# Layer 0 of a two-layer attention and MLP kernel: which tiles are transposed where, and when weight pieces are loaded

## The chip, the cores and the metric

The kernel runs on one core of a Trainium2 chip. The core has five engines that run side by side, each through its own list of instructions in order: TensorE (PE; its weight loads are shown as a separate row, PEld), VectorE (DVE), ScalarE (ACT), GpSimd (POOL) and SyncE (SP), which here only issues DMAs. They are held together by semaphores. The metric is the device time of one execution in microseconds (us), lower is better: 882.56 us, the median of three runs (882.15 to 882.82).

## The reference

`x` is 2048 rows of 448 numbers. Two layers with the same weights follow one another; in each

```
y   = layernorm(x);  q, k, v = split(y @ wqkv)            # 16 heads of 28
pq  = phi(q); pk = phi(k)                                  # phi(t) = (t+1 if t>0 else exp(t)) + 1e-6
kv  = sum over rows of pk^T v;  z = sum over rows of pk    # per head
x   = x + ((pq @ kv) / (pq . z + 1e-6)) @ wo
x   = x + gelu(layernorm(x) @ w1 + b1) @ w2 + b2           # w1: 448 x 1792, w2: 1792 x 448
```

The attention is linear: nothing of it is 2048 x 2048, but `kv` and `z` need all rows before the first output row can be made.

## The kernel before, in words

**Tiles and phases.** The rows are cut into 16 tiles of 128. A layer has three phases. Phase 1 takes the tiles one by one: normalise, project to k and q, and add k^T times the normalised rows into four accumulators (`G`; v itself is never formed). Phase 2 (`ORDER`, L494) makes from them the small matrices for the output and does the first block of four tiles. Phase 3 is the MLP of each block of four tiles, with the attention output of the next block woven in.

**Two pieces per number.** All large products are made from fp32 split in a rounded high piece and the remainder, each product being three matmuls (hi*hi, hi*lo, lo*hi). The split of a tile or a weight is a copy on ACT and a subtraction on DVE or POOL. A group `K`, `Q` or `G` of one tile is 11 matmuls of 448 columns.

**How a tile gets transposed.** The projections need the tile with its columns on the partitions. There are two ways. With `t < TURNED[l]` (L374), TensorE does it: `stage_b` (token `T`) issues four 128x128 transposes into a PSUM bank with tag `h`, which the q projection also uses, and `stage_x` (token `X`) splits it, ACT `XH` (L251) and DVE `XL` (L252). ACT first has to make a copy of the last 64 columns, twice (`tail`, L387). With `t >= TURNED[l]` the tile is "turned": DVE transposes blocks of 32x32 into a `sq` tile shared by two rows' tiles (`turn`, L277 and L278; tokens `tu`, or `v7` for tile 7), SP stores that to DRAM (`store_sq`, L283), and after the store has landed SP reads it back in four permuted DMAs (`spread`, L289, token `sp`); `stage_x` then splits the result, ACT `XH` (L295) and DVE `XL` (L296). Before, tiles 0 to 5 of layer 0 go through TensorE and 6 to 15 are turned. Layer 1 turns all of its tiles.

**The order is written by hand.** Phase 1 is a list of steps, one per tile; `STEPS` (L502) gives the tokens of a step, `STEP` (L501) the default. A token's instructions go to their engines' queues in that order. In step t: `K` and `Q` project tile t, `T` and `X` transpose and split tile t+1, `G` accumulates tile t-1, `qp` finishes q of tile t-1 and stores it, `kp`, `kh`, `kl` finish k, `s` splits the normalised tile for `G`. `a`, `n` are the statistics (with a power on POOL, L203) and the normalisation, for the tiles that `NORM[0][t]` lists, or for the tile in the token (`a5`). `ld` loads x up to the last tile of `NORM[0][t+2]`. Steps 9 to 15 have no `Q`: those q projections fill phase 2.

**Weights in the background.** In layer 0, w1 and w2 arrive in 32 pieces, 20 of them in phase 1. Token `bg` calls `background(n, m)` (L359): it first splits up to m pieces that are waiting (ACT copy L341, L344 or L352, then POOL subtraction L342, L345 or L353), then has SP issue n more loads. A piece lands in one of two buffers (`stg`), so a load waits in SP's queue until the POOL subtraction of the piece two before it is done. All DMAs of the kernel are in SP's one queue, in the order of the tokens: behind such a load wait the x loads, the spreads, the stores of q, and at the end of phase 1 the loads of `pq` that phase 2 starts with. `BG` (L523) is n for each step.

**Phase 2 begins** with `Q ld1 z ld0 ld2 qz0 qz1 G gt qs1 Q Qp kv qs0 tq1 ...`, ahead of which `background(0)` splits what is still waiting. `z` is a matmul and an ACT operation (`zb`, L622); `gt` four ACT copies of the accumulators (L632); `qz` a product of `pq` and `zb` on POOL (L693); `qs` a DVE chain (L699 to L704); `kv` 32 matmuls (L640); `tq1` the first transposes of `pq` (L711).

Of the kernel before, what the change touches and what calls it, by code (L numbers as in the profile page):

```python
# [9 lines left out]
F32 = mybir.dt.float32  # L10
# [12 lines left out]
def linear_attn_mlp_kernel(  # L23
# [12 lines left out]
    pe, act, dve, pool, sp = nc.tensor, nc.scalar, nc.vector, nc.gpsimd, nc.sync  # L36
# [8 lines left out]
    G = 112  # L45
# [6 lines left out]
    work = ctx.enter_context(tc.tile_pool(name="work", bufs=2))  # L52
# [136 lines left out]


    def ln_bn(xs):
        st = work.tile([128, 6], F32, name="bst", tag="bst", bufs=2)
        dve.bn_stats(st, xs)
        return st

    def ln_stats(xs, st=None):
        st = ln_bn(xs) if st is None else st
        mv = work.tile([128, 2], F32, name="bmv", tag="bmv", bufs=2)
        dve.bn_aggr(mv, st)
        ve = work.tile([128, 1], F32, name="bve", tag="bve", bufs=2)  # L200
        dve.tensor_scalar(ve, mv[:, 1:2], 1e-5, None, op0=OP.add)  # L201
        rs = work.tile([128, 1], F32, name="brs", tag="brs", bufs=2)
        pool.tensor_tensor(rs, ve, mhalf, op=OP.pow)  # L203
        return xs, mv, rs

# [28 lines left out]
    def block(key):  # L234
        if key not in blocks:
            blocks[key] = Block()
        return blocks[key]
# [10 lines left out]
    def split_x(key, j):  # L248
        tp = tps.pop((key, j))
        hi, lo = blocks[key].pieces(j)  # L250
        act.copy(hi, tp)  # L251
        dve.tensor_sub(lo, tp, f(hi))  # L252
# [19 lines left out]
    def turn(x, key, t):  # L272
        x = x[:, :D]
        if (key, t // 2) not in squares:
            squares[key, t // 2] = half("sq")
        sq = squares[key, t // 2].rearrange("p (m c u n) -> p c m u n", m=4, c=4, n=32)[:, :, :, t % 2]
        dve.transpose(sq[:, :3], x[:, :TL].rearrange("p (c m n) -> p c m n", c=3, n=32))  # L277
        dve.transpose(sq[:, 3].rearrange("p (u m) n -> p u m n", u=2),  # L278
                      x[:, TL:].rearrange("p (m n) -> p m n", n=32)[:, None].to_broadcast([128, 2, 2, 32]))
# [44 lines left out]
    def bg_pieces():  # L324
        n = 0

        def stage():
            nonlocal n
            n += 1
            if n <= LATE:  # L330
                return t512("xn", 2, "stg")[:, :D]
            return t448(f"W{5 + n % 2}", 1, "stg")

        for fc in range(4):
            sl = slice(fc * D, (fc + 1) * D)
            for c in range(4):
                s = stage_piece(w1[:, sl], c, sp, stage())

                def go(c=c, s=s, sl=sl):
                    if c < 3:  # L340
                        act.copy(w1h[:, c, sl], s)  # L341
                        pool.tensor_tensor(w1l[:, c, sl], s, f(w1h[:, c, sl]), op=OP.subtract)  # L342
                    else:
                        act.copy(w1x[:, sl], s)  # L344
                        pool.tensor_tensor(w1x[64:128, sl], s[64:128], f(w1x[64:128, sl]), op=OP.subtract)  # L345
                yield go
        for i in range(NF):
            s = stage()
            sp.dma_start(s, w2[i * 128:(i + 1) * 128, :])

            def go(i=i, s=s):
                act.copy(w2h[:, i], s)  # L352
                pool.tensor_tensor(w2l[:, i], s, f(w2h[:, i]), op=OP.subtract)  # L353
            yield go

    bg = bg_pieces()
    bg_wait = []

    def background(n, m=NF):  # L359

        for g in bg_wait[:m]:
            bg_wait.pop(0)()
        for _ in range(n):
            g = next(bg, None)
            if g is not None:
                bg_wait.append(g)
# [4 lines left out]
    sts = {}  # L371


    TURNED = (6, 0)  # L374
    tails = {}

    def stage_a(l, t):
        sts[l, t] = ln_stats(xt.pop((l, t)))

    def stage_n(l, t):  # L380
# [3 lines left out]
        xns[l, t] = xs  # L384
        if t < TURNED[l]:
            d = tails[l, t] = work.tile([128, 128], F32, name="tail", tag="tail", bufs=2)
            act.copy(d.rearrange("p (u n) -> p u n", u=2), xs[:, None, TL:].to_broadcast([128, 2, 64]))  # L387

    def stage_t(l, t):
        if t >= TURNED[l]:  # L390
            turn(xns[l, t], ("a", l, t // 4), t % 4)
            if t % 2:
                store_sq(("a", l, t // 4), t % 4 // 2)

    def stage_sp(l, t):
        if t >= TURNED[l]:
            block(("a", l, t // 4))
            spread(("a", l, t // 4), t % 4 // 2)

    def stage_b(l, t, tag="h"):  # L400
        if t < TURNED[l]:
            transpose_x(xns[l, t], tails.pop((l, t)), ("a", l, t // 4), t % 4, tag)

    def stage_x(l, t):
        key = ("a", l, t // 4)
        if t < TURNED[l]:
            split_x(key, t % 4)
# [67 lines left out]
    def stage_g(l, t, acc):  # L475
# [26 lines left out]
    STEPS = {  # L502
# [8 lines left out]
    }  # L511
    NORM = (
        ((2,), (3,), (5, 6), (7,), (8, 9), (10,), (11,), (12,), (13,), (14,), (15,)),
        ((5,), (6,), (7,), (8,), (9,), (10,), (11,), (12, 13), (14,), (15,)),
    )

# [3 lines left out]
        "qa1 qb1 qa2 qb2 Q00 Q10 Q01 Q11 Q02 Q12 s0 a2 kp0 qa3 qb3 kh0 n2 kl0 kp1 Q03 Q13"  # L520
    )
    PRE = 5
    BG = [0, 1, 2, 1, 1] + [2] * 4 + [1] * 7  # L523
    LATE = sum(BG)
    loaded = {0: 3}

# [25 lines left out]
    def phase1(l, tr):  # L552
        za = consts.tile([128, D], F32, name="za", tag="za")
        acc = []
        load_to(l, 4 if l == 0 else NORM[l][1][-1])
        if l == 0:
            launch(za)
            load_to(l, NORM[l][2][-1])
        for t in range(l == 0, NT):
            norm = NORM[l][t] if t < len(NORM[l]) else ()  # L560
            for tok in STEPS.get((l, t), STEP).split():
                if tok[1:].isdigit() and tok[0] in "anv":
                    {"a": stage_a, "n": stage_n, "v": stage_t}[tok[0]](l, int(tok[1:]))
                elif tok == "q1":
                    stage_qphi(1)
                elif tok == "sp":
                    for key, h in list(stored):
                        block(key)
                        spread(key, h)
                elif tok == "ld" and t + 2 < len(NORM[l]):  # L570
                    load_to(l, NORM[l][t + 2][-1])
                elif tok == "a":
                    for u in norm:
                        stage_a(l, u)
                elif tok == "n":
                    for u in norm:
                        stage_n(l, u)
                elif tok == "tu":
                    for u in norm:
                        stage_t(l, u)  # L580
                elif tok == "T" and t + 1 < NT:
                    stage_b(l, t + 1, "acc" if t == 1 else "h")
                elif tok == "X" and t + 1 < NT and (l == 0 or t + 1 >= 4):
                    stage_x(l, t + 1)
                elif tok == "K":
                    stage_k(l, t)
                elif tok == "qp":
                    stage_qphi()
                elif tok == "kp":
                    stage_kphi(l, t)  # L590
                elif tok == "kh":
                    stage_kh(l, t)
                elif tok == "kl":
                    stage_kl(l, t, za)
                elif tok == "s":
                    stage_s(l, t)
                elif tok == "G" and t >= 1:
                    acc = acc or [bank("acc", 4, f"G{c}")[:, :D] for c in range(4)]
                    stage_g(l, t - 1, acc)
                elif tok == "bg" and l == 0:  # L600
                    background(BG[t], 1 if t >= 9 else 2)
                elif tok == "Q" and t < DEFER:
                    stage_q(l, t)
            if t == 11:
                tr.wv = stage_square(wqkv[:, 2 * D:])
            if t == 13:
                trans_load(l, tr)
        return za, acc
# [309 lines left out]
    for l in range(LAYERS):  # L918
# [11 lines left out]
        def pre(j):  # L930
# [6 lines left out]
            Q=lambda j: stage_q(l, fill.pop(0)), Qp=lambda j: fill_qphi(), Qv=lambda j: stage_qphi(j or 9),  # L937
            Qa=lambda j: stage_q(l, fill.pop(0), tag="acc"), G=lambda j: stage_g(l, NT - 1, acc),
            ld=lambda j: (load_pq(l, 0, j), load_x(l, j)), z=lambda j: trans_z(tr, za), gt=lambda j: trans_gt(tr, acc),
# [5 lines left out]
            st=lambda j: store_sq(("m", l, 0), 0), sp=lambda j: spread(("m", l, 0), 0), pre=pre, b=biases)  # L945
        for tok in ORDER.split():
            name, j = tok.rstrip("0123456789"), int("0" + tok.lstrip("abcdefghijklmnopqrstuvwxyzQTG"))
# [6 lines left out]
        for b in range(NB):  # L954
# [6 lines left out]
            for i in range(NF):  # L961
# [12 lines left out]
                elif l + 1 < LAYERS:  # L974
# [4 lines left out]
                    if i in (3, 4, 6, 7, 8):  # L979
                        t = (3, 4, 6, 7, 8).index(i)  # L980
# [36 lines left out]
```

## Time and profile before

| | |
|---|---|
| median of 3 runs | 882.56 us |
| the profiled execution's own time | 883.35 us |
| its span in the trace | 881.6 us |
| PE / PEld busy | 873.4 us (99%) / 770.4 us (87%) |
| DVE / ACT / POOL busy | 491.0 / 341.8 / 220.9 us |
| layer 0, first `T` of step 1 to the `z` matmul (trace time 17.53 to 105.84) | 88.31 us |
| layer 0, `z` matmul to the first MLP matmul (105.84 to 143.30) | 37.46 us |
| the same in layer 1 (538.95 to 574.00) | 35.05 us |

Times in the trace start at the span's begin. A line of a group or of the timeline names the kernel's line, the engine, the operation and "output<-inputs" by the program's tile names; "idle before <-X" says how long the engine stood still before it and whose event ended that. Matmuls are pipelined: one of 448 columns is shown with 0.36 us, but follows the one before by 0.20 us, so start times tell more than busy times. Waits for operands show best in the weight-load row (PEld). K of step t starts at: 20.24 (t=2), 27.41, 34.57, 41.81, 48.97, 56.95, 63.77, 70.59 (t=9), 75.14, 79.68, 85.34, 89.89, 94.44, 99.16 (t=15).

### The profile page before, as it was taken

How to read it: one execution, taken by the hardware profiler on the slowest of the kernel's cores; microseconds unless marked ns; L12 is line 12 of the kernel's file. 1: busy time of each engine (PE TensorE's matmuls, PEld its weight loads, DVE VectorE, ACT ScalarE, POOL GpSimd, SP SyncE). 2: the span in 40 equal slices, each digit the busy share in tenths (PEclk: the TensorE clock that was granted, in tenths of full speed). 3: DMA queues.
4: the chain of work that ended last, by engine and by line, in shares of the span. 5: the costliest groups of instructions: out<-in, count | busy, mean ns of one | idle time of the engine just before them, and what ended most of it. 6: DMA issues, size and time to landing. Idle time of an engine off the chain costs nothing.

```text
span 881.6 us, 11694 instructions
## 1 busy us (share of the span) xinstructions
PE 873.4 (99%) x4174; PEld 770.4 (87%) x4174; DVE 491.0 (56%) x957; ACT 341.8 (39%) x601; POOL 220.9 (25%) x250
## 2 busy tenths in 40 slices
PE   9999999999999999999999999999999999999998
PEld 8988878888888888888899999888888888888887
DVE  6978476658554634225568776765574473432112
ACT  5666644423223321333355564342232233223221
POOL 5556542325002102002222243220220140140000
PEclk9999999999999999999999999999999999999999
DMA  5475636624412402051136543253332323111001
GB/s 160 141 223 194 185 97 200 203 78 135 148 59 80 163 16 83 14 178 48 48 114 184 175 145 95 89 185 99 99 118 90 119 66 132 48 49 42 1 1 42
DMA packets 64202, 95.81 MB, mean 109 GB/s; under 512 B 8976, under 2 KB 59152, under 8 KB 64144
## 3 DMA queue, kind: packets, MB, share of 16 engines
q1 hardware_dynamic: 64144, 95.06, 34.6%
q8 instruction: 33, 0.54, 0.3%
q14 instruction: 25, 0.20, 0.1%
HBM read 56.70 MB, written 35.13 MB: 104 GB/s over the span
## 4 chain that ended last, share of the span: by engine, by line
PE 83%; DVE 2%; issue 1%; ACT 0%; POOL 0%; DVEq 0%; POOLq 0%
PE y L820 10%; PE y L818 10%; PE y L819 10%; PE hp L802 9%; PE hp L801 9%; PE hp L800 9%; PE hp L804 3%; PE hp L803 3%; PE op L743 2%; PE op L742 2%; PE op L744 2%; PE psq L308 1%; PE psq L306 1%; PE psq L307 1%; PE psk L307 1%; PE G L481 1%
## 5 line engine op out<-in xcount | busy, mean ns | idle before, releaser
L810 DVE TENSOR_TENSOR gl<-g,gh 128x512 fp32r<-128x512 f32 x112 | 82.7, 738 | 300.4 <-ACT gh L809 300.4
L806 ACT ACTIVATE g<-hp,b1s 128x512 f32<-128x512 f32 x112 | 77.1, 688 | 407.1 <-PE hp L804 405.0
L820 PE MATMUL y<-w2h,gl 128*128 128x448 f32 x448 | 163.7, 365 | 0.0
L819 PE MATMUL y<-w2l,gh 128*128 128x448 f32 x448 | 163.6, 365 | 0.0
L818 PE MATMUL y<-w2h,gh 128*128 128x448 f32 x448 | 163.6, 365 | 0.0
L802 PE MATMUL hp<-XL,w1h 128*128 128x512 f32 x336 | 131.2, 391 | 0.6 <-DVE XL L252 0.5
L801 PE MATMUL hp<-XH,w1l 128*128 128x512 f32 x336 | 131.5, 391 | 0.0
L800 PE MATMUL hp<-XH,w1h 128*128 128x512 f32 x336 | 131.3, 391 | 0.0
L203 POOL TENSOR_TENSOR brs<-bve,mhalf 128x1 f32<-128x1 f32 x64 | 38.9, 607 | 284.6 <-DVE bve L201 281.4
L818 PEld LDWEIGHTS y<-w2h,gh 128*128 128x128 f32 x448 | 84.1, 188 | 9.0
L819 PEld LDWEIGHTS y<-w2l,gh 128*128 128x128 f32 x448 | 84.1, 188 | 8.4
L820 PEld LDWEIGHTS y<-w2h,gl 128*128 128x128 f32 x448 | 84.2, 188 | 6.6
L802 PEld LDWEIGHTS hp<-XL,w1h 128*128 128x128 f32 x336 | 63.1, 188 | 15.0 <-issue 1.4
L801 PEld LDWEIGHTS hp<-XH,w1l 128*128 128x128 f32 x336 | 63.1, 188 | 11.2
L800 PEld LDWEIGHTS hp<-XH,w1h 128*128 128x128 f32 x336 | 63.1, 188 | 11.0
L809 ACT CAST gh<-g 128x512 fp32r<-128x512 f32 x112 | 69.7, 622 | 3.6
L693 POOL TENSOR_TENSOR pz<-pq,zb 128x448 f32<-128x448 f32 x32 | 36.6, 1148 | 87.2 <-DVE dn L699 69.4
L416 POOL TENSOR_TENSOR xnl<-x,xnh 128x384 fp32r<-128x384 f32 x32 | 35.6, 1114 | 73.7 <-ACT xnh L415 45.5
L296 DVE TENSOR_TENSOR XL<-sp,XH 128x512 fp32r<-128x512 f32 x52 | 45.2, 875 | 8.2 <-ACT XH L295 8.2
L803 PE MATMUL hp<-XH,w1x 128*128 128x512 f32 x112 | 43.6, 389 | 0.0
L804 PE MATMUL hp<-XL,w1x 128*128 128x512 f32 x112 | 43.6, 389 | 0.0
L762 POOL TENSOR_TENSOR x<-x,b2b 128x448 f32<-128x448 f32 x32 | 41.9, 1332 | 0.0
(146 smaller groups left out, 1563.2 us busy)
## 6 DMA issues: line engine op xcount, KB each, us to landing
x<-in_A_x_dram SPq DMA_DIRECT2D x32, 224.0 KB, 3.7
pq_d<-eq SPq DMA_DIRECT2D x32, 224.0 KB, 2.9
pq<-pq_d SPq DMA_DIRECT2D x32, 224.0 KB, 3.3
sq_m<-sq SPq DMA_DIRECT2D x14, 512.0 KB, 2.8
sp<-sq_m SPq DMA_DIRECT2D x56, 128.0 KB, 3.0
x<-x_d SPq DMA_DIRECT2D x32, 224.0 KB, 3.6
sq_a<-sq SPq DMA_DIRECT2D x13, 512.0 KB, 2.9
sp<-sq_a SPq DMA_DIRECT2D x52, 128.0 KB, 3.0
```

The lines of the kernel that those rows point to most:

```text
L296: eng.tensor_tensor(lo.rearrange("p (c i n) -> p c i n", c=4, n=32), x, f(h), op=OP.subtract)
L800: pe.matmul(o, w1h[:, c, s], x.moving(x.hi, c), start=(c == 0), stop=False)
L801: pe.matmul(o, w1l[:, c, s], x.moving(x.hi, c), start=False, stop=False)
L802: pe.matmul(o, w1h[:, c, s], x.moving(x.lo, c), start=False, stop=False)
L803: pe.matmul(o, w1x[:, s], x.moving(x.hi, 3), start=False, stop=False)
L804: pe.matmul(o, w1x[:, s], x.moving(x.lo, 3), start=False, stop=True)
L806: act.activation(g, hp, AF.Gelu_apprx_tanh, bias=b1s[:, i:i + 1])
L809: act.copy(gh, g)
L810: dve.tensor_sub(gl, g, f(gh))
L818: pe.matmul(acc[j], gh[:, s], w2h[:, i], start=first, stop=False)
L819: pe.matmul(acc[j], gh[:, s], w2l[:, i], start=False, stop=False)
L820: pe.matmul(acc[j], gl[:, s], w2h[:, i], start=False, stop=last)
```

## The change

Five edits, all in phase 1 of layer 0:

- `TURNED` goes from 6 to 8: tiles 6 and 7 are transposed by TensorE (in steps 5 and 6) and no longer turned, stored and spread.
- Steps 3 and 4 get new token lists. Step 3 has the statistics of 7 and 8 and the normalisation of 6 only, no turn and no spread. Step 4 has the statistics of 9, the normalisation of 7, 8, 9, and the turn, store and spread of 8 and 9 (that pair was in step 4 before, too).
- `NORM[0]` lists tile 8 with tile 7, so x of tile 8 is loaded in step 1, not in step 2.
- The small tiles of the statistics get three buffers, not two.
- `BG`: pieces loaded in step t were 1, 2, 1, 1, then 2 in steps 5 to 8, then 1 in steps 9 to 15. They become 1, then 2 in steps 2 to 7, 1 in steps 8 to 14, and 0 in step 15. At most one piece is split in a step from step 8 on (before from step 9), so that from then on a piece waits two steps for its split. Twenty pieces in phase 1 either way; before, two of them are left for `background(0)`, after it one.

```diff
-        st = work.tile([128, 6], F32, name="bst", tag="bst", bufs=2)
+        st = work.tile([128, 6], F32, name="bst", tag="bst", bufs=3)
...
-    TURNED = (6, 0)
+    TURNED = (8, 0)
...
-        (0, 3): "qp K T X s n6 v6 kp a7 kh kl n7 v7 G bg Q ld sp",
+        (0, 3): "qp K T X s a7 kp kh n6 kl a8 G bg Q ld",
+        (0, 4): "qp K T X s a9 kp kh n7 n8 kl n9 v8 v9 G bg Q ld sp",
...
-        ((2,), (3,), (5, 6), (7,), (8, 9), (10,), (11,), (12,), (13,), (14,), (15,)),
+        ((2,), (3,), (5, 6), (7, 8), (9,), (10,), (11,), (12,), (13,), (14,), (15,)),
...
-    BG = [0, 1, 2, 1, 1] + [2] * 4 + [1] * 7
+    BG = [0, 1] + [2] * 6 + [1] * 7 + [0]
...
-                    background(BG[t], 1 if t >= 9 else 2)
+                    background(BG[t], 1 if t >= 8 else 2)
```

More of the change, by code (lines that the diff above doesn't have):

```diff
@@ L197, in ln_stats @@
         st = ln_bn(xs) if st is None else st
-        mv = work.tile([128, 2], F32, name="bmv", tag="bmv", bufs=2)
+        mv = work.tile([128, 2], F32, name="bmv", tag="bmv", bufs=3)
         dve.bn_aggr(mv, st)
-        ve = work.tile([128, 1], F32, name="bve", tag="bve", bufs=2)
+        ve = work.tile([128, 1], F32, name="bve", tag="bve", bufs=3)
         dve.tensor_scalar(ve, mv[:, 1:2], 1e-5, None, op0=OP.add)
-        rs = work.tile([128, 1], F32, name="brs", tag="brs", bufs=2)
+        rs = work.tile([128, 1], F32, name="brs", tag="brs", bufs=3)
         pool.tensor_tensor(rs, ve, mhalf, op=OP.pow)
```

## The prediction

> **What bounds the kernel now.** I read the page first, then who waits for whom on PE's weight loads, then the stretches, then the queues of the engines that PE waited for.
>
> ```profile
> span 881.6 us, 11694 instructions
> ...
> PE 873.4 (99%) x4174; PEld 770.4 (87%) x4174; DVE 491.0 (56%) x957; ACT 341.8 (39%) x601; POOL 220.9 (25%) x250
> ```
>
> PE sets the time, and a gain can only be PE work taken out or a PE wait ended. The waits of PEld from 17 to 120 us are nearly all that the kernel has after its start:
>
> ```profile
> PEld tq L711 <- DVE pq L704: 2.0, 1, 2.0
> PEld G L482 <- DVE kl L440: 1.3, 3, 0.5
> PEld psk L308 <- DVE XL L296: 0.9, 2, 0.5
> PEld G L481 <- ACT kh L433: 0.9, 2, 0.4
> PEld psk L306 <- ACT XH L295: 0.7, 1, 0.7
> ```
>
> The stretches say how much that is (us; PE, PEld, DVE, ACT, POOL busy; clock; DMA):
>
> ```profile
> 17.53:105.84 88.31, 87.34 (x424) 77.36 (x423) 68.62 (x141) 58.09 (x114) 50.20 (x62) 1.00 0.58 176
> 460.92:536.71 75.79, 75.79 (x375) 70.25 (x374) 58.19 (x117) 44.65 (x83) 25.61 (x37) 1.00 0.52 159
> ...
> 105.84:143.30 37.46, 35.64 (x193) 30.53 (x191) 26.40 (x55) 16.31 (x35) 13.84 (x14) 1.00 0.41 123
> 538.95:574.00 35.05, 35.05 (x193) 30.80 (x192) 26.96 (x56) 16.39 (x34) 11.29 (x12) 1.00 0.29 91
> ```
>
> Layer 1's phase 1 (second row) is 34 groups of 11 matmuls without a wait: 2.23 us each. Layer 0's (first row) is 37 such groups, 82.5 us, and four tiles of transposes. A tile of transposes costs, by its start times,
>
> ```profile
> 29.64 0.49 PE L246 MATMUL tp<-ident,x 128*128 128x128 f32 x3
> 29.96 0.27 PE L246 MATMUL tp<-ident,tail 128*128 128x128 f32 x1
> 29.99 0.45 PE L481 MATMUL G<-kh,xnh 128*128 128x448 f32 x1
> 30.28 0.37 PE L482 MATMUL G<-kl,xnh 128*128 128x448 f32 x1
> ```
>
> 0.35 us to the next matmul and 0.09 that this one is longer than 0.20: 0.44. So layer 0 needs 82.5 + 1.8 = 84.2 and takes 88.3: 4.1 us are lost. Rows three and four: the same 193 matmuls take 2.4 us longer in layer 0. ACT's timeline shows who is late:
>
> ```profile
> 48.30 0.62 ACT L295 CAST XH<-sp 128x512 fp32r<-128x512 f32 x1 [3.67 <-DMA sp<-sq_a]
> ...
> 77.91 0.57 ACT L344 CAST w1x<-stg 128x448 fp32r<-128x448 f32 x1 [2.35 <-DMA stg<-in_B_w_dram]
> ...
> 108.28 0.57 ACT L352 CAST w2h<-stg 128x448 fp32r<-128x448 f32 x1 [3.01 <-DMA stg<-in_B_w_dram]
> ```
>
> First, ACT stands for tile 6 until its spread lands. Groups K6, G5 and the Q before them (46.27 to 54.68) take 8.41 us, not 6.69: 1.7 lost. Second, ACT stands for piece 12 of the weights, loaded in step 8 and split in step 9; XH of tile 11 is queued behind it, and K11 and G10 (79.68 to 85.34) lose 1.2. Third, the last piece, loaded in step 15, lands only at 108.28, with `zb` and `gt` queued behind it on ACT; and SP held that load until POOL had split piece 18, so that the loads of `pq` went out late:
>
> ```profile
> 106.23 0.38 SPq L689 DMA_DIRECT2D pq<-pq_d  x1
> ...
> 116.19 0.65 PE L711 MATMUL tq<-ident,pq 128*112 128x128 f32 x4 [1.82 <-DVE pq L704]
> ```
>
> The other 1.2 of phase 1: G13 waits 0.2 at 96.71, and from 54.68 to 96.71 the 16 groups without a wait take 2.27 each, not 2.23 (0.65 in all; nothing in the trace names a cause; it begins and ends at a wait); the rest lies in four groups before that.
>
> **The change, part by part.**
>
> Tiles 6 and 7 on TensorE: 2 x 0.44 = +0.9 us of PE, on the path. Bounds: 0.35 (the start distance alone) to 0.55 a tile, as 0.1 is what a touching wait on a bank adds to a group (Q4 at 39.50). The Trainium skill (TensorE: Matmul & The Clock Gate, Part 4: PE-mode transpose) gives about 275 ns for one 128x128 transpose; the rows show that duration too (0.27), but starts 0.1 apart. By the page's figure eight in a row would be 2.2 us and the sum 1.3 us worse.
>
> Beside it, per tile, ACT has a tail copy more (0.30, L387) and DVE two transposes fewer (0.57 and 0.27); DVE's split stays at 0.68. The wait of tile 6 goes: its transposes need only n6, in step 3, two steps earlier. Minus 1.7. What is late next there? Tile 8. Its store and spread stay in step 4. By DVE's rows step 4 starts with q of tile 3 at about 37.8 (ACT gives it then), and holds 6.9 us: q and split 1.2, statistics 0.95, k 0.55, three normalisations 1.6, kl and za 1.1, four transposes 1.5. Its store goes out near 44.7 (46.38 before), with no older spread in SP's queue, and the spread lands near 51; X of tile 8, in step 7, ran at 60.29. Cover of about 9 us. The bank that `T` takes makes Q5 and Q6 wait for q of the tile before on DVE: about 44.6 against Q5 at 46.8, 1.6 or more spare.
>
> Pieces two a step from step 2. Steps 4 and 5 split one more each: ACT 0.56, POOL 1.16. The wait that matters is ACT's for a landing; loads of step 3 go out when POOL has split pieces 2 and 3, which moves from 36.7-39.1 to some 37.6-40.0, because POOL's power of tile 8 is now queued ahead; they land by 42.7 (2.6 us in the rows of issues from 100 to 113), ACT wants them at 41.5 and 42.1. Steps 6 to 8 before are the same pattern: ACT waited 1.29 at 58.21 and 0.64 at 70.58, and PE lost nothing, as X of the next tile is done some 2 us before K needs it. I take 0; if that cover is gone, the row at 48.3 prices it: 1.7 a step. The x loads, q stores and spreads queued on SP behind the later loads are 1.2 us late, x loads wanted a step later; x of tile 8 goes ahead of the loads that wait (33 us before, 26 now). The third buffers cost nothing. POOL has 1.16 more beside DVE in two steps: L383 takes 0.50 alone and 1.20 at 21.16 beside L416, so up to 0.7 a normalisation, within the 1.6 spare. The Trainium skill (SBUF — State Buffer, SBUF: two separate sides) says that a GpSimd operation and certain DVE operations exclude each other for a whole instruction; the row agrees in kind (0.7 longer). By that, each of the two added splits could hold DVE for 1.16, 2.3 in all, of which no step gets more than its spare 1.6.
>
> Split a step later. Step 8 splits only piece 12 (loaded in step 7, in the pattern that cost PE nothing); from step 9 on a piece has landed long before. The wait at 77.91 goes: minus 1.2. Late next there: tile 14's spread. ACT waited 1.97 for it at 92.84; its store hangs on turn 15, behind XL of tile 12, which was itself late through the same ACT wait. Without it turn 15 comes some 2.9 earlier and K14 1.2 earlier, so it keeps more cover than now. Minus 0.2 at G13, which followed from that.
>
> No load in step 15. Piece 20 takes piece 19's place: issued at 101.86, split from 104.70 on ACT, POOL done at 106.9. `zb` then follows the `z` matmul (106.5, was 108.75), and `pq` goes out at 102.3, not 106.23. With the slowest landing shown (4.7), POOL's products start by 108, not 111.78; `tq1`'s `pq` is ready near 112.2, before PE gets there at 114.2. Layer 1 has the same chain with nothing in the background: 2.4 us less at most. I take 2.2, as `pq` may land 0.7 after `zb`. Bounds 0 (another wait in its place) and 2.4. The MLP's own pieces start from the same token and move with PE; no wait of PE shows there.
>
> The slow groups: 0 to -0.65, and up to +0.9 if all groups got slow (0.04 x 37, less the 0.65 already there). I take -0.4, as the waits that they lie between go.
>
> Sum: +0.9 - 1.7 - 1.2 - 0.2 - 0.4 = -2.6 in phase 1 (at most -3.2: 88.31 to 82.5 + 2.6) and -2.2 behind it: -4.8 us. The profiled execution, 883.35 (span 881.6), goes to 878.5, its span to 876.8. It stands 0.8 above the median of the runs; from that, 882.56 - 4.8 = 877.8.
>
> **The rivals.** *The end of phase 1 keeps its wait*, because `pq` lands late or POOL is not free: only -2.6, 880.0. For it: the three `pq` loads of that place took 4.5 in the median; against it: 4 us are gained at their issue. *A wait in phase 1 stays or comes elsewhere* (tile 8, step 11): one of 1.2 to 1.7 left, 879.0 to 879.5. *Nothing much*: both together, 0.9 paid for the transposes; about 881.5, within 0.2%. *Slower*: the doubled pieces block ACT in steps 4 to 7. Mechanism: a piece lands more than about 3 us after ACT reaches it, XH of the next tile is queued behind it, K waits. The price is that of 48.3, 1.7 a step; three steps (5.1) use up the gain, four give +2.0, 884.6. For it: the wait at 77.91 is just this; against: that was a step of 4.5 us, these have 7.1, and the same pattern in steps 6 to 8 cost nothing.
>
> **How the numbers follow.** The forecast 0.60, the first rival 0.08, the second 0.12, nothing much 0.08, slower 0.12. A measurement here can't tell changes under 0.2%, 1.8 us, from none. Faster 0.80, same 0.08, slower 0.12. Range: from 876.7 (3.2 + 2.4 = 5.6 less, and 0.3 as the runs scatter) to 881.0, which takes in the first two rivals and leaves out a little under 0.2.
>
> **What would show it.** Right: no PE wait for XH of tile 6 nor for XL of tile 11; ACT's copy of the last piece before `zb` with `zb` within 1 us of the `z` matmul; no wait at `tq`; `z` to the first MLP matmul near 35.2; the stretch from the first `T` to `z` near 85.7. Wrong: ACT waits for `stg` in steps 4 to 7 with K waiting behind, or a wait for `sp` at tile 8 or 14.

## The result: slower, and not where the change was made

The changed kernel takes 884.87 us (median of 9 runs), the kernel before 882.56: a ratio of 1.0026, 95% interval 1.0016 to 1.0036. The forecast was 877.8, in a range from 876.7 to 881.0.

The page of the changed kernel's profile begins

```profile
span 883.1 us, 11676 instructions
...
PE 877.8 (99%) x4182; PEld 773.0 (88%) x4182; DVE 489.9 (55%) x953; ACT 343.5 (39%) x603; POOL 220.8 (25%) x250
```

It has 1.5 us more of span, 4.4 us more of PE time, for 8 matmuls more. The waits of PEld from 17 to 120 us, the view that carried the prediction, are nearly gone:

```profile
PEld mp L651 <- issue: 1.2, 6, 0.2
PEld G L482 <- DVE kl L440: 0.5, 1, 0.5
PEld tq L712 <- issue: 0.4, 2, 0.2
PEld G L481 <- ACT kh L433: 0.3, 1, 0.3
```

No XH of tile 6, no XL, no `pq`. The stretches of the changed kernel (length and PE, PEld, DVE, ACT, POOL busy; clock; DMA) are, in order, phase 1 from the first `T`, from `z` to the first MLP matmul, layer 0's MLP, layer 1's phase 1, and layer 1's MLP to the end:

```profile
18.09:104.04 85.95, 85.77 (x432) 78.72 (x431) 67.40 (x137) 59.44 (x116) 50.66 (x62) 1.00 0.58 177
104.04:139.10 35.06, 35.06 (x193) 30.80 (x191) 27.13 (x56) 16.96 (x35) 12.49 (x13) 1.00 0.41 116
139.10:445.87 306.77, 306.77 (x1421) 266.80 (x1420) 155.14 (x291) 101.19 (x165) 64.51 (x60) 1.00 0.31 99
445.87:537.29 91.42, 91.42 (x453) 84.70 (x451) 68.87 (x138) 50.98 (x93) 28.69 (x43) 1.00 0.52 161
572.35:883.10 310.75, 306.92 (x1421) 266.60 (x1419) 132.98 (x255) 88.64 (x140) 42.87 (x40) 1.00 0.24 77
```

The last three stretches of the kernel before, which the prediction didn't look at, in the same view:

```profile
143.30:447.54 304.24, 303.77 (x1422) 266.61 (x1420) 155.48 (x292) 101.47 (x166) 64.03 (x60) 1.00 0.32 100
447.54:538.95 91.41, 91.41 (x453) 84.72 (x452) 68.88 (x138) 51.01 (x93) 28.71 (x43) 1.00 0.52 161
574.00:881.60 307.60, 303.93 (x1421) 266.42 (x1419) 133.43 (x255) 88.78 (x141) 42.58 (x40) 1.00 0.24 77
```

So phase 1 gave 2.36 and the stretch behind it 2.40, together 4.76 us where 4.8 were forecast. Then layer 0's MLP took 2.53 more and layer 1's MLP 3.15 more, and the start up to the first `T` 0.56 more (it lies between 17.39 and 18.20 in the sixteen traces of this study, whatever the kernel: scatter). -4.76 + 2.53 + 3.15 + 0.56 = +1.5, the difference of the spans.

The MLP has the same instructions in the same order, a granted clock of 1.00 both times, and no more DMA. PE waits less in it, not more: in the kernel before it stood for XL at the start of layer 0's MLP,

```profile
144.40 0.47 PE L802 MATMUL hp<-XL,w1h 128*128 128x512 f32 x1 [0.47 <-DVE XL L252]
```

and that wait is gone. So by PE's busy time, the second number of a row, the two MLPs are slower by 3.00 (303.77 to 306.77) and 2.99 (303.93 to 306.92). They are slow evenly: the start times drift apart by 0.06 us in each step, through both layers. A step is 11 matmuls `hp` (512 columns) and 12 `y` (448 columns); by the start times of PE's matmuls, from the first of a group to the first of the next, mean of 54 groups in layer 0, `hp` takes 2.552 us and took 2.510, `y` 2.446 and 2.434. The groups of the changed kernel by line (mean ns in the last number)

```profile
L801 PE MATMUL hp<-XH,w1h 128*128 128x512 f32 x336 | 132.8, 395 | 0.0
L803 PE MATMUL hp<-XL,w1h 128*128 128x512 f32 x336 | 132.4, 394 | 0.0
...
L805 PE MATMUL hp<-XL,w1x 128*128 128x512 f32 x112 | 44.4, 397 | 0.0
```

and the same in the kernel before (each line one lower) say it too, 3 to 8 ns a matmul:

```profile
L800 PE MATMUL hp<-XH,w1h 128*128 128x512 f32 x336 | 131.3, 391 | 0.0
L802 PE MATMUL hp<-XL,w1h 128*128 128x512 f32 x336 | 131.2, 391 | 0.6 <-DVE XL L252 0.5
...
L804 PE MATMUL hp<-XL,w1x 128*128 128x512 f32 x112 | 43.6, 389 | 0.0
```

What can reach from an edit in phase 1 to the MLP? One thing is in the allocation that the program lists: the four small tags with three buffers, not two, take 4 x 32 bytes more of each partition, and everything allocated behind them lies 128 bytes higher: `tail`, the wk pieces, XH and XL, the wq pieces, gh, gl, g, kh, kl, `xn`. The x tiles, the S tiles and the w1 and w2 pieces, allocated ahead of them, stay. So the distance between XH and w1h, for one, changes from a multiple of 256 bytes (147520 - 5696 = 554 x 256) to 128 more.

### The profile page after: what moved, and what is told of

Read it like the earlier page. It is cut to its first block, busy times and chain, and to the rows that moved or that the text cites. A ratio compares the mean times of both kernels' runs of the same rounds, so it can differ in the third digit from the quotient of the medians.

```text
span 883.1 us, 11676 instructions
## 1 busy us (share of the span) xinstructions
PE 877.8 (99%) x4182; PEld 773.0 (88%) x4182; DVE 489.9 (55%) x953; ACT 343.5 (39%) x603; POOL 220.8 (25%) x250
## 4 chain that ended last, share of the span: by engine, by line
PE 96%; DMA 1%; DVE 1%; ACT 1%; issue 0%; SPq 0%; POOL 0%; DVEq 0%; ACTq 0%; POOLq 0%
PE y L820 10%; PE y L821 10%; PE y L819 10%; PE hp L801 9%; PE hp L803 9%; PE hp L802 9%; PE hp L805 3%; PE hp L804 3%; PE psq L308 2%; PE psq L307 2%; PE psq L306 2%; PE psk L307 2%; PE G L482 2%; PE G L483 2%; PE psk L308 2%; PE G L481 2%
```

## The experiments

### Is it the place of the tiles? The third buffers alone, and the old places

The first kernel is the one before with nothing but the third buffers:

```diff
-        st = work.tile([128, 6], F32, name="bst", tag="bst", bufs=2)
+        st = work.tile([128, 6], F32, name="bst", tag="bst", bufs=3)
```

(and the same for `bmv`, `bve`, `brs`).

> The kernel before with the third buffer of the four small statistics tiles and nothing else: every tile allocated behind them, XH, XL, wk, wq, gh, gl among them, lies 128 bytes higher, the w1 and w2 pieces and the x tiles stay. Theory P (place): the hp matmuls of the MLP, which take 2.55 us a group in the changed kernel and 2.51 before, are slower because of where the tiles lie. Then this kernel has the slow MLP and nothing that pays for it: an MLP step of 5.00 us and not 4.94, some 5.9 us over 882.6, about 888.5. Theory C (code): the instruction stream ahead of the MLP, longer by 8 matmuls, sets the pace of its fetch; then 882.6 and 4.94. Theory S (state): PE's pace is left by whatever wait came last, as in the slow groups of phase 1; then 882.6 and 4.94 too, since the waits are those of before.

Measured: 889.86 us, ratio 1.0090 (1.0076 to 1.0105). Its stretches from phase 1 on:

```profile
18.14:106.22 88.08, 86.54 (x424) 77.60 (x423) 68.76 (x141) 58.02 (x114) 50.15 (x62) 1.00 0.57 177
106.22:144.03 37.81, 35.69 (x192) 30.52 (x191) 26.52 (x55) 16.42 (x35) 13.86 (x14) 1.00 0.41 121
144.03:451.32 307.29, 306.92 (x1421) 266.79 (x1420) 155.30 (x292) 101.48 (x166) 64.53 (x60) 1.00 0.32 99
...
577.80:888.30 310.50, 306.94 (x1421) 266.62 (x1419) 132.96 (x255) 88.64 (x140) 42.88 (x40) 1.00 0.24 77
```

The first two are those of the kernel before, the MLPs those of the changed one (+3.05 and +2.90). Theory P holds, C and S fall for the MLP. The median is 1.4 above the 888.5 worked out for it.

The second kernel is the changed one with the small tiles elsewhere and all others at their addresses of before:

```diff
+    small = ctx.enter_context(tc.tile_pool(name="small", bufs=1))
...
+    work.tile([128, 64], F32, name="pad", tag="pad", bufs=1)
...
-        st = work.tile([128, 6], F32, name="bst", tag="bst", bufs=3)
+        st = small.tile([128, 6], F32, name="bst", tag="bst", bufs=3)
```

> The changed kernel, its four small tiles in a pool of their own at the end of the memory and 256 bytes left free where they were, so that every other tile lies at the address that it has in the kernel before. P: all of the MLP's loss comes back, 4.94 us a step, and the gain of phase 1 and of what follows it (4.76 us in the traces) is what is left: 877.8. C: as the changed kernel, 884.9 and 5.00. S: 884.9 too, as the waits are those of the changed kernel.

Measured: 878.74 us, ratio 0.9964 (0.9951 to 0.9977).

```profile
18.13:104.09 85.96, 85.77 (x432) 78.73 (x431) 67.42 (x137) 59.39 (x117) 50.67 (x62) 1.00 0.58 176
104.09:139.14 35.05, 35.05 (x193) 30.79 (x192) 27.27 (x56) 16.64 (x35) 12.55 (x13) 1.00 0.40 117
139.14:442.93 303.79, 303.79 (x1421) 266.50 (x1420) 154.52 (x291) 101.09 (x165) 65.00 (x60) 1.00 0.31 100
...
569.39:877.00 307.61, 303.82 (x1421) 266.39 (x1419) 133.23 (x255) 88.66 (x140) 42.75 (x40) 1.00 0.24 77
```

The phase-1 gain of the change, and the MLP of before. These two settle where the changed kernel's time went: the third buffers cost 6.1 us of its median (884.87 against 878.74). By the profiled executions this kernel is 4.6 us faster than the one before (883.35 to 878.74), by the medians of one comparison 3.7 (882.48 to 878.74): the profiled execution of before was 0.8 above its median.

### How far, and which tiles?

The other kernels are this one (or the changed one) with bytes left free at other places, each by one or two lines such as

```diff
+            if not blocks:
+                work.tile([128, 32], F32, name="gap1", tag="gap1", bufs=1)
             self.hi = work.tile([128, 2048], F32R, name="XH", tag="XH", bufs=2)
```

Distances first.

> The changed kernel with 128 bytes more left free behind the x and S tiles, so that the tiles lie 256 bytes above their places of before, not 128. P with a period of 256 bytes: 877.8 and 4.94. P with a longer period: 884.9 and 5.00, or another pace. C and S: 884.9.

> The changed kernel with 384 bytes more left free there, so that the tiles lie 512 bytes above their places of before. P with a period of 256 or 512 bytes: 877.8 and 4.94; with a longer one 884.9. C and S: 884.9.

> The changed kernel with the tiles behind the statistics 64 bytes above their places of before. If only a full 128 bytes hurts: 878.7 and 4.94 us a step. If any distance other than a multiple of 256 does: between that and 884.6, by distance half of the loss, 881.7.

> The same, 192 bytes up. If the loss goes by the distance from the nearest multiple of 256, as at 64 bytes. Should one of the two be faster than the old places, it is the better kernel; no theory here says so.

Then which tiles.

> The changed kernel with all tiles at their places of before, except XH and XL, the transposed tiles: these 128 bytes up, and what lies behind them 256 bytes up, a shift that cost nothing. Theory X: hp is slow because of where XH and XL lie, which it alone streams 128 columns at a time from four tiles: then 5.00 us an MLP step and about 884.6 (5.9 over the 878.7 of the old places). Theory B: it is the tiles behind them (gh, gl, g and so on, written and read by ACT and DVE beside the matmuls): then 4.94 and 878.7.

> The complement: XH and XL at their places of before, all that lies behind them 128 bytes up. X: 4.94 us a step and 878.7. B: 5.00 and 884.6.

> The changed kernel in the old order of places with 128 bytes left free ahead of everything, so that the w1 and w2 pieces are moved as far as XH and XL. If the place of XH and XL itself counts: 5.00 us a step and 884.6. If it is their place relative to the weights that are loaded into PE at the same time (both at 64 bytes past a multiple of 256 before, 128 apart in the changed kernel): 4.94 and 878.7.

> The old places with the w1 pieces alone moved 128 bytes against all other tiles (what lies behind them goes up 256, which cost nothing). Theory R: hp is slow where its two operands, the w1 piece that is loaded into PE and the XH or XL that streams through it, lie 128 bytes apart within 256; then hp takes 2.55 us a group, y keeps 2.43, an MLP step 4.99, and the time is 884 to 885. If XH and XL have to agree with some tile other than w1 (gh, gl, w2): hp 2.51 and 878.7.

> The same with the w2 pieces alone moved 128 bytes against all other tiles. R: hp keeps 2.51. For y, whose operands gh and w2 are then as far apart as with all the rest moved (where y took 2.446 against 2.433, and hp 2.53): between nothing (878.7) and half of the loss (881.7). If w2 is what XH and XL have to agree with: 884 to 885.

> The changed kernel with the w1 pieces and XH, XL moved 128 bytes together, all other tiles a multiple of 256 from their places of before. Theory R (hp goes by how far its two operands lie apart): hp 2.51 us a group and an MLP step of 4.94 to 4.97; 878.5 to 881, the upper end if the matmuls that pair XH with wk, or gh with XH's neighbours, then lose as they did with only the rest moved (882.6). If XH and XL have to agree with some other tile than w1, or w1 with another than XH: hp 2.55 or more and 884 to 893.

Measured (us; `hp` and `y` are a group of 11 and of 12 matmuls in layer 0's MLP, by start times as above, mean of 54; "rest" is what lies behind XL; distances are from the places of before, modulo 256 for tiles not named):

| moved | `hp` | `y` | layer 1, phase 1 | layer 1, MLP | median | ratio to before (95%) |
|---|---|---|---|---|---|---|
| nothing (old places) | 2.510 | 2.436 | 91.41 | 307.61 | 878.74 | 0.9964 (0.9951-0.9977) |
| X and rest 64 | 2.537 | 2.429 | 93.21 | 309.26 | 883.20 | 1.0014 (1.0004-1.0023) |
| X and rest 128 (the change) | 2.552 | 2.446 | 91.42 | 310.75 | 884.87 | 1.0026 (1.0016-1.0036) |
| X and rest 192 | 2.565 | 2.414 | 93.21 | 309.81 | 884.79 | 1.0032 (1.0022-1.0043) |
| X and rest 256 | 2.510 | 2.434 | 91.41 | 307.68 | 878.44 | 0.9961 (0.9946-0.9975) |
| X and rest 512 | 2.510 | 2.433 | 91.40 | 307.61 | 878.85 | 0.9960 (0.9948-0.9973) |
| everything 128 | 2.510 | 2.434 | 91.40 | 307.63 | 878.37 | 0.9955 (0.9938-0.9972) |
| w2 128 | 2.499 | 2.444 | 91.41 | 307.66 | 878.49 | 0.9961 (0.9946-0.9976) |
| X 128 | 2.552 | 2.453 | 91.80 | 311.12 | 886.41 | 1.0046 (1.0028-1.0063) |
| rest 128 | 2.526 | 2.447 | 91.57 | 309.32 | 882.61 | 1.0003 (0.9992-1.0013) |
| w1 128 | 2.570 | 2.477 | 93.20 | 313.94 | 892.88 | 1.0125 (1.0110-1.0140) |
| w1 and X 128 | 2.540 | 2.433 | 91.80 | 309.29 | 882.60 | 1.0000 (0.9990-1.0010) |

What follows. The loss repeats with a period of 256 bytes (256 and 512 cost nothing; 64, 128 and 192 all cost, so none of them is the period). It isn't an address as such: with everything moved by 128, the `hp` matmuls are back at 2.510. It is a distance between tiles. Moving w2 alone leaves the time as it is: `y` takes 0.010 us more than in the kernel before, and `hp` 0.011 less. Moving w1 alone against all others costs the most, more than the change itself; XH and XL alone cost `hp` what the change cost it. In both, `hp`'s own two operands end 128 apart, as theory R has it.

But R isn't all of it, and the times forecast with it and with theory X were missed. With w1 alone moved (884 to 885 forecast, 892.88 measured), `y` slows from 2.434 to 2.477 as well, though it doesn't read w1. With w1 and X moved together (878.5 to 881 forecast, 882.60 measured), `hp` should have been at 2.51, and is at 2.540. The rest alone (878.7 by X, 884.6 by B, 882.61 measured) makes `hp` 2.526, though no operand of `hp` is in it. Nor do 128 bytes between the two operands cost every matmul the same: in the rows "X 128" and "w1 and X 128" the K and Q groups of layer 1 have their operands, X and wk or wq, 128 apart too, and take 2.240 us, not 2.229. That is 0.5% more, where `hp` pays 1.7% with X alone moved.

So the place of w1 against X carries about half of what X alone costs (886.41, and 882.60 with w1 moved along; 878.74 with nothing moved). The other half goes with the place of both against other tiles, and I haven't found the pair. There may be none: with the rest alone moved, the 7th to the 11th matmul of `hp` follow one another by 0.227 us, as in the kernel before, and its loss lies in the six steps ahead of them and in the step to `y`. So it may come over from `y`, whose operands gh and w2 are then 128 apart; no run separates the two.

The two extreme rows in the view of stretches, layer 1's phase 1 and MLP, of the kernel with w1 alone moved

```profile
448.59:541.79 93.20, 93.20 (x452) 84.66 (x451) 68.87 (x138) 51.04 (x93) 28.45 (x43) 1.00 0.52 159
...
576.86:890.80 313.94, 310.16 (x1421) 266.82 (x1419) 132.70 (x255) 88.60 (x140) 42.79 (x40) 1.00 0.23 76
```

and of the one with everything moved:

```profile
442.42:533.82 91.40, 91.40 (x452) 84.72 (x451) 68.90 (x138) 51.03 (x93) 28.72 (x43) 1.00 0.53 161
...
568.87:876.50 307.63, 303.86 (x1421) 266.42 (x1419) 133.27 (x255) 88.69 (x140) 42.77 (x40) 1.00 0.24 78
```

Same instructions, same clock, no wait in the first row of either: PE is busy for the whole 93.20 and the whole 91.40.

### Does the pace carry over?

The first of these has a puzzle: layer 1's phase 1 doesn't read w1, and its tiles lie as they should, yet each of its groups takes 2.27 us, not 2.23. That is the pace of the "slow groups" that the prediction found in phase 1 of layer 0 and couldn't explain. The `y` groups of this kernel have it too: their matmuls start 0.207 us apart, as those of a group of 2.27 do, where in the kernel before it is 0.203. So the kernel with w1 moved, and a break of four matmuls of 128 columns ahead of that phase, whose result isn't used:

```diff
+        if l:
+            brk = bank("m", 2, "brk")
+            for _ in range(4):
+                pe.matmul(brk[:, :128], ones, ones, start=True, stop=True)
         za, acc = phase1(l, tr)
```

> The kernel with w1 alone moved 128 bytes (892.9), with four matmuls of 128 columns put between layer 0's MLP and layer 1's phase 1. There its groups took 2.27 us each without any wait, not 2.23, and w1 isn't read in that phase. If that pace is carried over from the MLP (theory S for that stretch): it ends at the break, layer 1's phase 1 takes 91.4 + 0.5 and not 93.2, and the time is 891.6. If it comes from where the tiles of that phase lie: it stays at 93.2 + 0.5, and 893.3.

Measured: 890.98 us, against 892.88 without the break (ratios to before 1.0101, 1.0086 to 1.0116, and 1.0125, 1.0110 to 1.0140, in two comparisons). The break, which the trace shows as eight matmuls, and the first matmul of the phase:

```profile
447.85 1.05 PE L929 MATMUL brk<-ones 128*128 128x128 f32 x8
448.66 0.45 PE L311 MATMUL psk<-wk,XH 128*128 128x448 f32 x1
```

Layer 1's phase 1, and the MLP behind it:

```profile
448.66:540.14 91.48, 91.48 (x454) 84.78 (x453) 67.99 (x137) 51.04 (x93) 28.15 (x41) 1.00 0.53 162
...
575.13:889.10 313.97, 310.16 (x1421) 266.78 (x1419) 132.59 (x255) 88.72 (x140) 42.82 (x40) 1.00 0.24 76
```

The break costs 0.8 us by its start times and the phase is 1.7 shorter. So the pace of that phase came from the MLP ahead of it: PE went on at a pace while matmul followed matmul, and four matmuls of another kind in between ended it. (The break also swaps the two PSUM banks that the K groups take by turns; without it the pace was the same 2.27 with either bank, and in the Q and G groups.) A wait alone doesn't always end it: in phase 1 of the kernel before, groups take 2.27 both ahead of the waits at K11 and G10 and behind them. So theory S, wrong as the cause of the changed kernel's MLP, is right for this stretch, and likely for `y` with w1 moved, which no run tests by itself.

### One part alone: the schedule of the pieces

```diff
-    BG = [0, 1, 2, 1, 1] + [2] * 4 + [1] * 7
+    BG = [0, 1] + [2] * 6 + [1] * 7 + [0]
...
-                    background(BG[t], 1 if t >= 9 else 2)
+                    background(BG[t], 1 if t >= 8 else 2)
```

> The kernel before with the new schedule of the weight pieces alone (loads per step, and one split a step from step 8), all tiles at their places. By the prediction's steps: the wait of K11 (1.2) and G13 (0.2) goes and the stretch from z to the first MLP matmul gives 2.2 to 2.4, tile 6 keeps its wait (1.7), the transposes are not paid: 882.5 less 3.6 to 3.8, about 878.8, and the MLP at 4.94 us a step. If the two parts need one another (the spread of 6 and 7 and the earlier pieces on the same queue), less: the wait for tile 6 grows, 880 or more.

Measured: 879.22 us, ratio 0.9967 (0.9956 to 0.9977), 3.1 us less than before in the same comparison. Its first two stretches, and ACT's wait for tile 6 on its timeline:

```profile
18.16:104.60 86.44, 85.96 (x424) 77.50 (x423) 68.62 (x141) 58.74 (x114) 51.08 (x62) 1.00 0.62 188
104.60:139.64 35.04, 35.04 (x192) 30.79 (x191) 27.28 (x56) 16.48 (x35) 12.58 (x13) 1.00 0.39 116
```

```profile
48.27 0.62 ACT L295 CAST XH<-sp 128x512 fp32r<-128x512 f32 x1 [1.05 <-DMA sp<-sq_a]
```

The stretch behind `z` gives its 2.4, phase 1 gives 1.9. Tile 6 keeps a wait: K6 and G5 take 2.51 and 2.80 us, 0.9 over two plain groups, where the kernel before lost 1.7 with the Q ahead of them. Its XH starts no earlier (48.27, was 48.30); PE comes to it later, as the first `T` started 0.6 later in this execution. So the pieces are worth most of the gain. What the transposes of tiles 6 and 7 on TensorE add, which cost 0.9 and end that wait, isn't shown: 878.74 at the same places against 879.22 here is within the intervals of the two comparisons.

## Why the prediction was wrong, point by point

**The step that failed** is "The third buffers cost nothing." It was the one edit costed without a row, and it cost 5.7 us in the profiled pair (2.53 + 3.15 in the MLPs; 6.0 by PE's busy time), 6.1 in the medians of the changed kernel with and without it, 7.4 when done alone. What was looked for was a wait, by the prediction's first rule that "a gain can only be PE work taken out or a PE wait ended"; that rule leaves out that the same matmuls can run at another pace. What the edit did was to move XH, XL and the tiles behind them by 128 bytes against the weights. None of the rivals had it. That the rival "slower" named 884.6, 0.3 from the median, is luck: its mechanism, K waiting behind pieces that land late in four steps, did not happen in one.

**Tiles 6 and 7 on TensorE**: +0.9 forecast; 0.36 to the next matmul and 0.08 on that one, twice, 0.88. The Trainium skill's 275 ns a transpose (TensorE: Matmul & The Clock Gate, Part 4: PE-mode transpose) is each one's duration here too (0.27), but they start 0.11 apart, so the row, not the product, was the price.

**The waits of K6 and K11**: gone, as said. **Pieces two a step**: ACT waited in step 4 for both of its pieces, and zero of it reached PE, as taken. ACT's timeline of the changed kernel, with two other waits that are left:

```profile
43.13 0.57 ACT L344 CAST w1x<-stg 128x448 fp32r<-128x448 f32 x1 [1.10 <-DMA stg<-in_B_w_dram]
44.35 0.57 ACT L341 CAST w1h<-stg 128x448 fp32r<-128x448 f32 x1 [0.65 <-DMA stg<-in_B_w_dram]
...
91.04 0.62 ACT L295 CAST XH<-sp 128x512 fp32r<-128x512 f32 x1 [2.32 <-DMA sp<-sq_a]
...
104.99 0.63 ACT L623 ACTIVATE zb<-zp,zc 128x448 f32<-128x448 f32 x1 [0.34 <-PE zp L621]
```

**Tile 14** was said to keep more cover than before, and G13 to gain 0.2. It lost 0.35: turn 15 ended 2.2 us earlier, not 2.9, K14 started 2.2 earlier, not 1.2, and the spread took a little longer (7.9 us from the store's issue to XH, was 7.4). G13 takes 2.79 us, was 2.45. A small term, with the wrong sign.

**No load in step 15**: -2.2 forecast, -2.40 measured; `zb` starts 0.95 after the `z` matmul does, and no wait stands at `tq`. **The slow groups**: -0.4 forecast; nearly all of the 0.65 went, since from K5 on every group is at 2.23 but K14, G13 and those right behind transposes.

**The MLP** was said to show no wait of PE. It had one, the 0.47 for XL at its start, and that went too, outside the sum.

Sum of phase 1 and the stretch behind: -4.8 forecast, -4.76 measured. That it fits so closely is partly luck: the terms missed both ways, and the five kernels of the table with the changed schedule and the MLP's old pace are 3.9 to 4.8 us shorter than before over the two stretches. At the old places the median is 878.74, inside the range and 0.9 above the forecast; the profiled execution of before, from which the terms were read, stood 0.8 above its median, which may be why.

## What to carry to other kernels

A change in the number or size of buffers moves every tile allocated behind it; compare the addresses before and after, and when a stretch that the change doesn't touch gets evenly slower with no wait in it, restore the addresses before looking for another cause. Here four buffers of 32 bytes turned a gain of 0.4% into a loss of 0.3%, and keeping the shift a multiple of 256 bytes gave the gain back. And where PE is busy for all of a span, compare the time that the same matmuls take, stretch by stretch, not only the waits.

## What the runs showed of the hardware that I had not expected

- The pace of matmuls depends on how far apart tiles lie, modulo 256 bytes: an `hp` group takes 2.499 to 2.510 us in the five good rows of the table and 2.510 in the kernel before, and 2.526 to 2.570 in the others, up to 2.4% more than before, with no wait in these groups. The Trainium skill (SBUF — State Buffer, SBUF: two separate sides) says that on the engines' side only the port pair shared by GpSimd and VectorE causes contention, and that PE never waits on anyone. These runs show a cost for PE that goes by the places of tiles; whether it is contention, and between which accesses, no run here shows.
- PE's pace persists: with w1 moved, groups of 11 matmuls ran at 2.27 us, not 2.23, through all 41 groups of layer 1's phase 1 without a wait, and with four short matmuls ahead of them they ran at 2.23. This rests on one trace of each kernel and on their medians. What sets the pace at a start is open, and so is what makes the second half of the placement's cost (`hp` 2.526 with the rest moved, 2.540 with w1 and X moved).
- The best kernels of the study are the change at any of the good places, 878.4 to 878.9 us, ratios 0.9955 to 0.9964: faster than both kernels.
